# A Fourier-filter and two-layer kernel: the first forward stage as sums and differences in 64-by-64 quarters, three stages' pieces gathered in one step, the second layer two steps behind

## The chip, the cores and the metric

The kernel runs on one core of one Trainium2 chip. The metric is device time in microseconds (us) of one execution; lower is better. "PE" is TensorE, "DVE" VectorE, "ACT" ScalarE, "POOL" GpSimd and "SP" SyncE, which here only issues DMAs.

## The reference

Eight sequences of 3008 rows and 256 columns are filtered in the frequency domain along the rows; the result goes through two matrix products with a PReLU between them.

```
X = np.fft.rfft(x, axis=1)                       # x: 8 x 3008 x 256
y = np.fft.irfft(X * (filt_r + 1j * filt_i), n=3008, axis=1)
h = y.reshape(24064, 256) @ w_in                 # 256 -> 2048
g = np.maximum(h, 0) + alpha * np.minimum(h, 0)
out = g @ w_out                                  # 2048 -> 256
```

## The kernel before

A 3008-point transform is split as 94 times 32. For each batch it has four stages.

- **Stage A** (`piece_a`, L148): a 94-point transform over the rows `n1`. `xs` holds 94 rows on partitions and 8 of the 32 values of `n2`, 256 columns each (a "chunk"; four chunks a batch). One piece is two matmuls (L155) with the stationary 94-by-96 table `wf1_s` and 512 columns each, into one `hps` tile in PSUM, which ACT copies to `asb`. Eight pieces a batch. `save_a` stores a chunk to `a_dram` in HBM, and `turn_a` reads it back transposed into `at`. Both are DMAs on SP's queue.
- **Stage B** (`piece_b`, L172): the 32-point transform as eight matmuls on 64-by-64 quarters of the array (L179), into the PSUM tile `psF`; then on DVE two products with the filter, `ww` (L186) and `uu` (L187). The halves of `ww` are swapped across partitions by four DMAs on POOL's queue: for batch 1 they accumulate straight into `uu` (L191), for later batches they land in `sw` (L193) and `piece_s` adds them on DVE (L198). Six pieces a batch.
- **Stage C** (`piece_c`, L200): the inverse 32-point transform, eight quarter matmuls (L210) into `hps`, copied by ACT to `v`. `turn_c` sends `v` through `v_dram` and reads it as `zt`. Six pieces a batch.
- **Stage D** (`pair_d`, L245): the inverse 94-point transform (L232) into `psF`, copied by ACT to `yT`, the input of the two layers. Eight pieces a batch.

The two layers work on blocks of 512 tokens (one of 384 in twelve). `up(j)` (L474), for 16 values of j, does two matmuls (L479) of the first layer; every second `up` fills an `hps` tile, ACT copies it to `gtb` (L488), and DVE applies the PReLU: two `tensor_scalar` into `m` (L491) and, once in four `up`, one add into `gtb` (L493). `down(q)` is one sixteenth of a block's second layer (a "unit": four matmuls, L510, three for the short block); ACT copies its result to `osb` (L515) and SP stores it (L461).

PSUM: `hps` has two buffers and serves stages A and C and `up`; `psF` has one, for B and D; `op` has two, for `down`. `gtb` is a ring of nine groups of four.

Batch 0 is transformed first, by a class of its own. All else is laid out by hand in 768 steps, one for each `up`. A dictionary `plan` names the pieces that each step does before its `up`; `plan_fft` (L524) fills it for a batch from lists of steps (`a_at`, `b_at`, `c_at`, `d_at` for the pieces, `ta` for `turn_a`, `x_at` for the next batch's loads, which `load_x` puts on POOL's queue). Batch b is filtered while batch b - 1 goes through the layers; stage A of a batch lies beside stages B and C of the batch before. The driver (L582) runs one unit of the block before in each step, after `up`, or before the pieces where the step has an A or C piece (`front`). Every engine executes its instructions in program order.

Of the kernel before, what the change touches and what calls it, by code (L numbers as in the profile page):

```python
# [1 line left out]

# [22 lines left out]
def _build_consts():  # L25

    n1, n2, p = np.arange(N1), np.arange(N2), np.arange(32)
    k1 = (2 * (np.arange(NK) // 2) + 24 * (np.arange(NK) % 2))[None, :] + np.arange(2)[:, None]
    k2 = np.where(p < 16, p, 47 - p)
    g = np.where(p < 16, 1.0, -1.0)  # L30

    a1 = 2 * np.pi * n1[:, None, None] * k1[None] / N1
    wf1 = np.stack([np.cos(a1), -np.sin(a1)], axis=2)
    scale = np.where((k1 == 0) | (k1 == 47), 1.0, 2.0)[None, :, None, :] / NFFT
    wi3 = (wf1 * scale).reshape(N1, 96).T
    wfx = wf1.transpose(0, 3, 1, 2).reshape(N1, 96)
    wf1 = wf1.reshape(N1, 96)

    kk = k1[:, :, None] + N1 * k2
    ang = 2 * np.pi * n2[:, None, None, None] * kk[None] / NFFT  # L40
    c, s = np.cos(ang), np.sin(ang)
    fwd = np.array([[c, -s * g], [s, c * g]])
    twf = fwd.transpose(3, 0, 2, 4, 1, 5).reshape(128, NK, 64)
    inv = np.array([[c, s], [-s * g, c * g]])
    inv = inv.reshape(2, 2, N2, 2, NK // 2, 2, 32).transpose(5, 0, 6, 4, 3, 1, 2)
    inx = np.stack([inv[:, 1], -inv[:, 0]], axis=1)
    return wf1, wfx, wi3, twf, inv.reshape(128, NK, 64), inx.reshape(128, NK, 64)


@with_exitstack  # L50
def kernel(
# [8 lines left out]
    out: bass.AP,  # L60
):
    nc = tc.nc
    names = ("wf1", "wfx", "wi3", "twf", "twi", "twx")
# [20 lines left out]


    wf1_s = konst.tile([N1, 96], FP16, name="wf1_s")
    wfx_s = konst.tile([N1, 96], FP16, name="wfx_s")
    wi3_s = konst.tile([96, N1], FP16, name="wi3_s")
    twf_s = konst.tile([128, NK, 64], FP16, name="twf_s")
# [17 lines left out]
                       ap=[[N2 * D, N1], [1, 8 * D]])  # L107

    def load_x(b, c):
        xs = p_x.tile([N1, 8 * D], FP16, name="xs")  # L110
        for r in (slice(0, 48), slice(48, N1)) :
            nc.gpsimd.dma_start(out=xs[r], in_=xrow(b, c)[r])  # L112
# [25 lines left out]
    class Fft:  # L138
# [3 lines left out]
            self.uw = {}  # L142

        def start_a(self):
            self.asb = p_fft.tile([96, N2, D], FP16, name="asb", tag="asb")
            self.at = p_fft.tile([128, NK, D], FP16, name="at")

        def piece_a(self, i):  # L148
            if i == 0:
                self.start_a()  # L150
            xs = xc[(self.b, i // 2)]
            ps = psH.tile([128, 2, 512], FP32, name="hps")
            for u in range(2):
                o = (i % 2) * 1024 + 512 * u
                nc.tensor.matmul(ps[0:96, u], wf1_s, xs[:, o : o + 512], start=True, stop=True)  # L155
            on_act(self.asb[:, 4 * i : 4 * i + 4].rearrange("p a d -> p (a d)"),
                   ps[0:96].rearrange("p a d -> p (a d)"))

        def save_a(self, c):
            s = slice(8 * c, 8 * c + 8)  # L160
            nc.sync.dma_start(out=a_dram[self.b, :, s], in_=self.asb[:, s])

        def turn_a(self, eng, ka=0, kb=NK):
            for par in range(2):
# [89 lines left out]
    def on_act(o, i):  # L254
        nc.scalar.activation(o, i, AF.Copy)  # L255
# [7 lines left out]
    class First(Fft):  # L263
# [9 lines left out]
        def piece_a(self, i, evict, wide):  # L273
            c, sh = i // 2, i % 2
            ps = banks(wide)
            for f in range(2):
                for u in range(4):
                    o = (4 * sh + u) * D + 128 * f
                    nc.tensor.matmul(ps[:, f, 96 * u : 96 * u + 96], xc[(0, c)][:, o : o + 128], wfx_s,
                                     start=True, stop=True)  # L280
            evict(self.am.rearrange("p (f m s) -> p f m s", f=2, s=N2)[:, :, :, 4 * i : 4 * i + 4],
                  ps[:, :, 0:384].rearrange("p f (s m) -> p f m s", s=4))
# [70 lines left out]
            evict(self.zt[:, 2 * i : 2 * i + 2].rearrange("p a d -> p (a d)"), pt[0:96, 0])  # L353

        def piece_t(self, i, evict):
            pt = banks(i == 4)
            self.turn(pt, i, 4)
            evict(self.zt[:, 4 * i : 4 * i + 4].rearrange("p (h a) d -> p h (a d)", h=2), pt[0:96])

# [43 lines left out]
    for kp in range(12):  # L403
        if kp < 10:
            f0.piece_b(kp + 2)
        if kp == 1:
            nc.vector.memset(twi_s[:, 16:24, 0:1], 0.0)
            tables(nc.sync, ("twi", "twx"), 16, 24)
            nc.sync.dma_start(out=wi3_s, in_=consts["wi3"].ap())
            nc.sync.dma_start(out=al16, in_=moe_alpha.rearrange("(j p) -> j p", p=128))  # L410
            nc.sync.dma_start(out=id32, in_=id32_d.ap())
            nc.sync.dma_start(out=wf1_s, in_=consts["wf1"].ap())
            nc.sync.dma_start(out=sgn_s, in_=sgn_d.ap())
# [105 lines left out]
    plan, front = {}, set()  # L519

    def put(step, fn, *args):
        plan.setdefault(step, []).append((fn, args))

    def plan_fft(b, a_at, ta, quarters, x_at, b_at, add, c_at, d_at):  # L524
        f = Fft(b)
        for i in range(8):
            put(a_at[i], f.piece_a, i)
            front.add(a_at[i])
        for c in range(4):
            put(a_at[2 * c + 1], f.save_a, c)  # L530
            if b + 1 < NB:
                put(x_at[c],
                    lambda b=b, c=c: xc.update({(b + 1, c): load_x(b + 1, c)}))
        for q in range(quarters):
            w = NK // quarters
            put(ta, f.turn_a, nc.sync, w * q, w * q + w)
# [4 lines left out]
        for q in range(6):  # L541
            put(c_at[q], f.piece_c, q)
            front.add(c_at[q])
            if q % 2 == 1:
                put(c_at[q] + 1, f.turn_c, q // 2)
# [22 lines left out]
    def d_steps(p):  # L568
        return [p + t for t in (91, 93, 104, 108, 116, 120, 140, 152)]

    plan_fft(1, range(12, 28, 2), 28, 4, (32, 40, 50, 56), range(36, 72, 6), 0, range(50, 86, 6),
             (94, 95, 98, 101, 111, 121, 142, 154))
    plan_fft(2, (48, 54, 60, 66, 72, 78, 82, 84), 90, 4, (57, 69, 81, 89),
             (106, 116, 126, 136, 148, 158), 7, (116, 126, 136, 148, 158, 172), d_steps(96))
    for b in range(3, NB):
        p = 96 * (b - 1)
        a_at = (10, 16, 22, 28, 34, 36, 44, 48) if b == 3 else (6, 10, 18, 22, 30, 34, 42, 46)
        a_at = [p - 96 + t for t in a_at]
        plan_fft(b, a_at, p - 32, 1, [a_at[2 * c + 1] + 2 for c in range(4)],
                 range(p + 2, p + 74, 12), 8, range(p + 14, p + 86, 12), d_steps(p))  # L580

    prev = None  # L582
    step = 0
    for p, t0, tn, _ in blocks:
        blk = Block(p, t0, tn)
        for j in range(16):
            ahead = step in front and prev is not None
            if ahead:
                prev.down(j)
            for fn, args in plan.pop(step, ()):  # L590
                fn(*args)
            blk.up(j)
# [38 lines left out]
```

## Time and profile before

| what | value |
|---|---|
| median of 3 runs | 783.1 us (782.0 to 789.35) |
| the profiled execution | 783.67 us, its span 781.9 us |
| granted TensorE clock | 0.999 |
| busy: PE, DVE, ACT, POOL | 767.8, 595.4, 587.0, 142.7 us |
| L510 and L479, the two layers | 435.8 and 434.2 us |
| L155, stage A | 33.6 us, 112 matmuls |
| L488 | 385.8 us, 384 instructions |
| L491 and L493 | 233.2 and 231.0 us |
| L186, L187, L198 | 51.1, 51.0, 24.6 us |

The span is the time from the first to the last instruction on the core; the execution's time is 1.8 us more. Busy time is a union over overlapping instructions, so a mean duration times a count can be more than it. For TensorE, whose matmuls overlap, the price of one is best read as the time from its start to the next one's. "Idle before" is the engine's idle time just ahead of an instruction, with what ended it.

### The profile page before, as it was taken

The numbers are of one execution on the slowest core, as the hardware profiler recorded it, in microseconds if no ns is written. First come the engines' busy times: TensorE is split into PE (matmuls) and PEld (weight loads), VectorE is DVE, ScalarE is ACT, GpSimd is POOL, SyncE is SP. The second block draws the span as 40 slices with busy tenths as digits, with TensorE's granted clock in tenths as the row PEclk, the third lists the DMA queues.
The fourth block names the chain that finished last, engine by engine and source line by source line (L and its number), as shares of the span: only waits on it lengthen the run. The fifth ranks groups of instructions, "written<-read, shape, count | busy, mean of one in ns | idle before, by whom it ended". The sixth has DMA issues, their size and how long they took to land.

```text
span 781.9 us, 16069 instructions
## 1 busy us (share of the span) xinstructions
PE 767.8 (98%) x6349; PEld 509.8 (65%) x6349; DVE 595.4 (76%) x1117; ACT 587.0 (75%) x673; POOL 142.7 (18%) x270
## 2 busy tenths in 40 slices
PE   7989999999999999999999999999999999999998
PEld 4646666666666666666666666766666666766666
DVE  3778975788868887787867888688887888666664
ACT  4787786888778877788777887788776877677664
POOL 7520661132102211122201221021111122000000
PEclk9999999999999999999999999999999999999999
DMA  9995799657744657465593565734475233511112
GB/s 171 175 236 149 111 216 219 168 134 173 144 134 101 158 125 152 132 144 114 143 210 80 126 142 126 177 82 108 116 150 135 55 82 95 147 37 28 42 41 54
DMA packets 95179, 100.38 MB, mean 128 GB/s; under 512 B 11184, under 2 KB 83008, under 8 KB 94912
## 3 DMA queue, kind: packets, MB, share of 16 engines
q1 hardware_dynamic: 80480, 69.98, 34.3%
q0 software_dynamic: 14624, 29.38, 21.5%
q8 instruction: 49, 0.80, 0.4%
q14 instruction: 26, 0.21, 0.1%
HBM read 55.28 MB, written 46.66 MB: 130 GB/s over the span
## 4 chain that ended last, share of the span: by engine, by line
PE 94%; DMA 2%; ACT 2%; DVE 1%; POOL 1%; issue 0%; ACTq 0%; POOLq 0%
PE hps L479 41%; PE op L510 41%; PE hps L155 3%; PE psF L232 3%; PE psF L179 2%; PE hps L210 1%; DMA xs<-in_x_dram 1%; ACT gtb L488 1%; DMA zt<-v_dram 1%; ACT v L255 1%; PE psF L347 1%; DMA filt_s<-in_filt_r_dram 0%; POOL xs L112 0%; PE op L325 0%; DVE uu L302 0%
## 5 line engine op out<-in xcount | busy, mean ns | idle before, releaser
L488 ACT ACTIVATE gtb<-hps 128x1024 f16<-128x1024 f32 (+1 forms) x384 | 385.8, 1005 | 133.2 <-PE hps L479 132.4
L510 PE MATMUL op<-wout_s,gtb 128*128 128x256 f16 x3008 | 435.8, 273 | 0.1
L479 PE MATMUL hps<-yT,win_s 128*128 128x512 f16 (+1 forms) x1536 | 434.2, 375 | 1.6 <-ACT gtb L488 1.4
L510 PEld LDWEIGHTS <-gtb 128*128 128x128 f16 x3008 | 293.8, 98 | 168.6 <-issue 0.6
L491 DVE TENSOR_SCALAR m<-gtb,alm_s 128x512 f16<-128x512 f16 (+1 forms) x768 | 233.2, 346 | 149.3 <-ACT gtb L488 148.1
L493 DVE TENSOR_TENSOR gtb<-gtb,m 128x2048 f16<-128x2048 f16 (+1 forms) x192 | 231.0, 1203 | 10.1
L479 PEld LDWEIGHTS <-win_s 128*128 128x128 f16 x1536 | 142.7, 98 | 60.9 <-issue 14.5
L193 POOL DMA_DIRECT2D sw<-ww x144 | 71.2, 502 | 388.5 <-DVE ww L186 377.7
L255 ACT ACTIVATE asb<-hps 96x1024 f16<-96x1024 f32 x56 | 57.1, 1020 | 13.7 <-PE hps L155 13.3
L515 ACT ACTIVATE osb<-op 128x512 f32<-128x512 f32 (+1 forms) x97 | 56.2, 579 | 5.6 <-issue 2.8
L255 ACT ACTIVATE yT<-psF 128x752 f16<-128x752 f32 x59 | 47.0, 797 | 10.0 <-PE psF L232 9.9
L255 ACT ACTIVATE v<-hps 128x1024 f16<-128x1024 f32 (+1 forms) x43 | 43.4, 1010 | 13.6 <-PE hps L210 13.2
L112 POOL DMA_DIRECT2D xs<-in_x_dram x64 | 38.2, 702 | 76.0 <-PE hps L155 69.7
L186 DVE TENSOR_TENSOR ww<-psF,filts_s 128x1024 f16<-128x1024 f32 x42 | 51.1, 1218 | 0.0
L187 DVE TENSOR_TENSOR uu<-psF,filt_s 128x1024 f16<-128x1024 f32 x42 | 51.0, 1215 | 0.0
L155 PE MATMUL hps<-xs,wf_s 94*96 94x512 f16 x112 | 33.6, 381 | 0.6 <-ACT asb L255 0.6
L232 PE MATMUL psF<-wi_s,zt 96*128 96x94 f16 x500 | 31.2, 205 | 1.7 <-DMA zt<-v_dram 1.4
L232 PEld LDWEIGHTS <-zt 96*128 96x128 f16 x512 | 28.5, 98 | 4.8 <-DMA zt<-v_dram 1.7
L191 POOL DMA_DIRECT2D uu<-ww x24 | 19.3, 1229 | 32.9 <-DVE uu L187 27.2
L198 DVE TENSOR_TENSOR uu<-uu,sw 128x1024 f16<-128x1024 f16 x36 | 24.6, 685 | 0.2 <-DMA sw<-ww 0.2
L179 PE MATMUL psF<-at,twf_s 64*64 64x256 f16 x336 | 17.3, 281 | 0.0
L210 PE MATMUL hps<-uu,twi_s 64*64 64x256 f16 x336 | 16.6, 272 | 0.0
(68 smaller groups left out, 168.7 us busy)
## 6 DMA issues: line engine op xcount, KB each, us to landing
out_dram<-osb SPq DMA_DIRECT2D x160, 128.0 KB
a_dram<-asb SPq DMA_DIRECT2D x28, 384.0 KB
v_dram<-v SPq DMA_DIRECT2D x84, 128.0 KB
zt<-v_dram SPq DMA_DIRECT2D x28, 384.0 KB
sw<-ww POOLq DMA_DIRECT2D x144, 64.0 KB, 2.3
at<-a_dram SPq DMA_DIRECT2D x20, 384.0 KB
xs<-in_x_dram POOLq DMA_DIRECT2D x32, 192.0 KB, 4.7
xs<-in_x_dram POOLq DMA_DIRECT2D x32, 184.0 KB, 5.6
```

What stands on the lines that cost most here:

```text
L155: nc.tensor.matmul(ps[0:96, u], wf1_s, xs[:, o : o + 512], start=True, stop=True)
L186: nc.vector.tensor_mul(ww, px, fs)
L187: nc.vector.tensor_mul(uu, px, f)
L193: nc.gpsimd.dma_start(out=sw[o : o + 32], in_=ww[i : i + 32])
L232: nc.tensor.matmul(ps[:, m], self.zt[:, 8 * g + 4 * mh + m, dh * 128 : dh * 128 + 128], wi3_s, start=True, stop=True)
L255: nc.scalar.activation(o, i, AF.Copy)
L479: nc.tensor.matmul(self.hps[:, j % 2, 0:tn], win_s[:, kt, j * 128 : (j + 1) * 128], yT[:, kt, self.t0 : self.t0 + tn], start=(kt == 0), st ...
L488: nc.scalar.activation(g[:, 2 * i : 2 * i + 2], self.hps[:, :, 0:tn], AF.Copy)
L491: nc.vector.tensor_scalar(m[:, 2 * i + h], g[:, 2 * i + h], 0.0, a, OP.min, OP.mult)
L493: nc.vector.tensor_add(g, g, m)
L510: nc.tensor.matmul(self.op[:, si - s0], self.gts[k][:, 128 * si : 128 * si + 128], wout_s[:, k], start=(si == s0 and k == 0), stop=(si == ...
L515: nc.scalar.activation(osb[:, 0:m], self.op[:, 0:m], AF.Copy)
```

## The change

1. **Stage A of batches 2 to 7 is split by parity.** Rows n and n + 47 of the 94-point transform differ only in sign for odd frequencies. `load_halves` loads rows 0 to 46 into a tile `lo` and rows 47 to 93 into another, `hi` (48 rows each, one to spare; two DMAs, on POOL's queue as before). On DVE, `less` writes `lo - hi` to partitions 64 to 110 of `lo`, and `plus` writes `lo + hi` over partitions 0 to 46. `piece_q` then does four matmuls of 512 columns on the four 64-by-64 quarters, with the 47-by-48 tables `wfq_s`: rows 0 to 46 give the even frequencies, rows 64 to 110 the odd, and the two column halves take two of the four `n2` of the piece. The result fills 128 partitions of `hps` in place of 96. `save_q` stores a chunk with two DMAs in place of one. Batch 1 keeps `piece_a`.
2. **The plan is new.** Within a step the order is C, B, A. From batch 3 on, stage A pieces mostly stand in steps that hold a B and a C piece too. The saves come one step later. Each load has three steps in `x_at`: the load, `less` and `plus`.
3. **The driver draws units from a queue.** In a step with n pieces that use `hps` it does n units before the pieces and n after them, and none after `up`; in odd steps away from such pieces it leaves the unit out while the queue holds fewer than 18 - j, so that the second layer falls up to two steps behind and is then drawn ahead.
4. `piece_t(2)` of batch 0 takes an `hps` buffer and `piece_t(4)` a `psF` one, the other way round from before.

```diff
+    def load_halves(b, c):
+        lo, hi = (p_x.tile([128, 8 * D], FP16, name="xs") for _ in range(2))
+        nc.gpsimd.dma_start(out=lo[0:48], in_=xrow(b, c)[0:48])
+        if b + 1 < NB:
+            nc.gpsimd.dma_start(out=hi[0:48], in_=bass.AP(
+                tensor=x.tensor, offset=x.offset + (b * NFFT + 47 * N2 + 8 * c) * D, ap=[[N2 * D, 48], [1, 8 * D]]))
...
+        def less(self, c):
+            lo, hi = xc[(self.b, c)]
+            nc.vector.tensor_tensor(lo[64:111], lo[0:47], hi[0:47], OP.subtract)
+
+        def plus(self, c):
+            lo, hi = xc[(self.b, c)]
+            nc.vector.tensor_tensor(lo[0:47], lo[0:47], hi[0:47], OP.add)
+
+        def piece_q(self, i):
...
+            ps = psH.tile([128, 2, 512], FP32, name="hps")
+            for h in range(2):
+                o = 1024 * h + 512 * u
+                for par in range(2):
+                    r = slice(64 * par, 64 * par + 47)
+                    nc.tensor.matmul(ps[64 * h : 64 * h + 64, par], wfq_s[r], xs[r, o : o + 512],
+                                     start=True, stop=True)
+            on_act(self.asb.rearrange("p (r c w) -> p r c w", r=2, c=4)[:, :, c, 512 * u : 512 * u + 512], ps)
+
+        def save_q(self, c):
+            for h in range(2):
+                nc.sync.dma_start(
...
-            pt = banks(i == 4)
+            pt = banks(i == 2)
...
     def plan_fft(b, a_at, ta, quarters, x_at, b_at, add, c_at, d_at):
         f = Fft(b)
...
+        for q in range(6):
+            put_h(c_at[q], f.piece_c, q)
+            if q % 2 == 1:
+                put(c_at[q] + 1, f.turn_c, q // 2)
         for q in range(6):
             put(b_at[q], f.piece_b, q, not add)
             if add:
                 put(b_at[q] + add, f.piece_s, q)
...
+        for i in range(8):
+            put_h(a_at[i], f.piece_q if x_at else f.piece_a, i)
+        for c in range(4):
+            put(a_at[2 * c + 1] + 1, f.save_q if x_at else f.save_a, c)
+            if x_at:
+                x0, x1, x2 = x_at[c]
+                put(x0, lambda b=b, c=c: xc.update({(b, c): load_halves(b, c)}))
+                put(x1, f.less, c)
+                put(x2, f.plus, c)
...
-    plan_fft(2, (48, 54, 60, 66, 72, 78, 82, 84), 90, 4, (57, 69, 81, 89),
-             (106, 116, 126, 136, 148, 158), 7, (116, 126, 136, 148, 158, 172), d_steps(96))
+    plan_fft(2, (48, 54, 60, 62, 66, 68, 74, 80), 90, 4,
+             ((32, 40, 44), (38, 50, 56), (55, 63, 64), (63, 70, 72)),
+             (106, 116, 126, 136, 148, 158), 7, (116, 126, 136, 148, 158, 170), d_steps(96))
     for b in range(3, NB):
         p = 96 * (b - 1)
-        a_at = (10, 16, 22, 28, 34, 36, 44, 48) if b == 3 else (6, 10, 18, 22, 30, 34, 42, 46)
-        a_at = [p - 96 + t for t in a_at]
-        plan_fft(b, a_at, p - 32, 1, [a_at[2 * c + 1] + 2 for c in range(4)],
+        if b == 3:
+            a_at = (100, 106, 112, 116, 126, 136, 148, 158)
+            x_at = ((70, 88, 97), (84, 102, 109), (108, 119, 123), (118, 130, 142))
+        else:
+            a_at = range(p - 118, p - 22, 12)
+            x_at = [(t - 34, t - 18, t - 6) for t in a_at[::2]]
+            if b == 4:
+                a_at = (170, *a_at[1:])
+        plan_fft(b, a_at, p - 28 if b > 3 else 166, 1, x_at,
                  range(p + 2, p + 74, 12), 8, range(p + 14, p + 86, 12), d_steps(p))
...
+    def pop(n):
+        for _ in range(n):
+            if units:
+                blk, q = units.popleft()
+                blk.down(q)
...
         for j in range(16):
-            ahead = step in front and prev is not None
-            if ahead:
-                prev.down(j)
+            n = psum.get(step, 0)
+            if step < 40:
+                pop(1 if n else 0)
+            else:
+                pop(n)
             for fn, args in plan.pop(step, ()):
                 fn(*args)
+            if step >= 40:
+                pop(n)
             blk.up(j)
-            if prev is not None and not ahead:
-                prev.down(j)
+            if n:
+                last = step
+            else:
+                soon = any(t in psum for t in range(step + 1, step + 14))
+                if not (step >= 40 and step % 2 and step - last > 2 and soon and len(units) < 18 - j):
+                    pop(1)
             step += 1
```

More of the change, by code (lines that the diff above doesn't have):

```diff
@@ L1 @@
+from collections import deque
 from contextlib import ExitStack
@@ L36, in _build_consts @@
     wfx = wf1.transpose(0, 3, 1, 2).reshape(N1, 96)
+    wfq = np.zeros((2, 64, 64))
+    wfq[:, :47, :48] = wf1[:47].transpose(1, 0, 2, 3).reshape(2, 47, 48)
+    wfq = wfq.reshape(128, 64)
     wf1 = wf1.reshape(N1, 96)
@@ L46, in _build_consts @@
     inx = np.stack([inv[:, 1], -inv[:, 0]], axis=1)
-    return wf1, wfx, wi3, twf, inv.reshape(128, NK, 64), inx.reshape(128, NK, 64)
+    return wf1, wfx, wfq, wi3, twf, inv.reshape(128, NK, 64), inx.reshape(128, NK, 64)
 @with_exitstack
@@ L62 @@
     nc = tc.nc
-    names = ("wf1", "wfx", "wi3", "twf", "twi", "twx")
+    names = ("wf1", "wfx", "wfq", "wi3", "twf", "twi", "twx")
     consts = {n: nc.inline_tensor(np.ascontiguousarray(v).astype(np.float16), name="c_" + n)
@@ L86 @@
     wf1_s = konst.tile([N1, 96], FP16, name="wf1_s")
+    wfq_s = konst.tile([128, 64], FP16, name="wfq_s")
     wfx_s = konst.tile([N1, 96], FP16, name="wfx_s")
@@ L109, in load_x @@
     def load_x(b, c):
-        xs = p_x.tile([N1, 8 * D], FP16, name="xs")
-        for r in (slice(0, 48), slice(48, N1)) :
+        xs = p_x.tile([128, 8 * D], FP16, name="xs")
+        for r in (slice(0, 48), slice(48, N1)):
             nc.gpsimd.dma_start(out=xs[r], in_=xrow(b, c)[r])
         return xs
+    def load_halves(b, c):
[5 more added lines that the diff above has]
+        else:
+            nc.gpsimd.dma_start(out=hi[0:32], in_=xrow(b, c)[47:79])
+            nc.gpsimd.dma_start(out=hi[32:47], in_=xrow(b, c)[79:94])
+        return lo, hi
     def load_filt(eng, dst, ha, hb):
@@ L144, in start_a @@
         def start_a(self):
-            self.asb = p_fft.tile([96, N2, D], FP16, name="asb", tag="asb")
+            self.asb = p_fft.tile([128, N2 * D], FP16, name="asb", tag="asb")
             self.at = p_fft.tile([128, NK, D], FP16, name="at")
@@ L154, in piece_a @@
                 o = (i % 2) * 1024 + 512 * u
-                nc.tensor.matmul(ps[0:96, u], wf1_s, xs[:, o : o + 512], start=True, stop=True)
-            on_act(self.asb[:, 4 * i : 4 * i + 4].rearrange("p a d -> p (a d)"),
-                   ps[0:96].rearrange("p a d -> p (a d)"))
+                nc.tensor.matmul(ps[0:96, u], wf1_s, xs[0:N1, o : o + 512], start=True, stop=True)
+            on_act(self.asb[0:96, 1024 * i : 1024 * i + 1024], ps[0:96].rearrange("p a d -> p (a d)"))
         def save_a(self, c):
             s = slice(8 * c, 8 * c + 8)
-            nc.sync.dma_start(out=a_dram[self.b, :, s], in_=self.asb[:, s])
+            nc.sync.dma_start(out=a_dram[self.b, :, s].rearrange("r s d -> r (s d)"),
+                              in_=self.asb[0:96, 2048 * c : 2048 * c + 2048])
+        def less(self, c):
[5 more added lines that the diff above has]
+        def piece_q(self, i):
+            if i == 0:
+                self.start_a()
+            c, u = i // 2, i % 2
+            xs = xc[(self.b, c)][0]
+            ps = psH.tile([128, 2, 512], FP32, name="hps")
[9 more added lines that the diff above has]
+                nc.sync.dma_start(
+                    out=a_dram[self.b, :, 8 * c + 4 * h : 8 * c + 4 * h + 4].rearrange(
+                        "(r k) s d -> k r (s d)", r=2),
+                    in_=self.asb[64 * h : 64 * h + 48].rearrange("p (r c w) -> p r c w", r=2, c=4)[:, :, c])
         def turn_a(self, eng, ka=0, kb=NK):
@@ L278, in piece_a @@
                     o = (4 * sh + u) * D + 128 * f
-                    nc.tensor.matmul(ps[:, f, 96 * u : 96 * u + 96], xc[(0, c)][:, o : o + 128], wfx_s,
+                    nc.tensor.matmul(ps[:, f, 96 * u : 96 * u + 96], xc[(0, c)][0:N1, o : o + 128], wfx_s,
                                      start=True, stop=True)
@@ L412 @@
             nc.sync.dma_start(out=wf1_s, in_=consts["wf1"].ap())
+            nc.sync.dma_start(out=wfq_s, in_=consts["wfq"].ap())
             nc.sync.dma_start(out=sgn_s, in_=sgn_d.ap())
@@ L517, in down, with put_h @@
                         store(self.p, self.t0 + 128 * (s0 + lane), osb, lane)
-    plan, front = {}, set()
+    plan, psum = {}, {}
     def put(step, fn, *args):
         plan.setdefault(step, []).append((fn, args))
+    def put_h(step, fn, *args):
+        put(step, fn, *args)
+        psum[step] = psum.get(step, 0) + 1
     def plan_fft(b, a_at, ta, quarters, x_at, b_at, add, c_at, d_at):
         f = Fft(b)
[L526 to L536, printed above, removed]
+        for q in range(6):
+            put_h(c_at[q], f.piece_c, q)
+            if q % 2 == 1:
+                put(c_at[q] + 1, f.turn_c, q // 2)
         for q in range(6):
@@ L540, in plan_fft @@
                 put(b_at[q] + add, f.piece_s, q)
[L541 to L545, printed above, removed]
+        for i in range(8):
[7 more added lines that the diff above has]
+                put(x2, f.plus, c)
+        for q in range(quarters):
+            w = NK // quarters
+            put(ta, f.turn_a, nc.sync, w * q, w * q + w)
         for i in range(8):
@@ L569, in d_steps @@
         return [p + t for t in (91, 93, 104, 108, 116, 120, 140, 152)]
-    plan_fft(1, range(12, 28, 2), 28, 4, (32, 40, 50, 56), range(36, 72, 6), 0, range(50, 86, 6),
+    plan_fft(1, range(12, 28, 2), 28, 4, None, range(36, 72, 6), 0, range(50, 86, 6),
              (94, 95, 98, 101, 111, 121, 142, 154))
-    plan_fft(2, (48, 54, 60, 66, 72, 78, 82, 84), 90, 4, (57, 69, 81, 89),
-             (106, 116, 126, 136, 148, 158), 7, (116, 126, 136, 148, 158, 172), d_steps(96))
+    plan_fft(2, (48, 54, 60, 62, 66, 68, 74, 80), 90, 4,
+             ((32, 40, 44), (38, 50, 56), (55, 63, 64), (63, 70, 72)),
+             (106, 116, 126, 136, 148, 158), 7, (116, 126, 136, 148, 158, 170), d_steps(96))
     for b in range(3, NB):
         p = 96 * (b - 1)
-        a_at = (10, 16, 22, 28, 34, 36, 44, 48) if b == 3 else (6, 10, 18, 22, 30, 34, 42, 46)
-        a_at = [p - 96 + t for t in a_at]
-        plan_fft(b, a_at, p - 32, 1, [a_at[2 * c + 1] + 2 for c in range(4)],
+        if b == 3:
[7 more added lines that the diff above has]
+        plan_fft(b, a_at, p - 28 if b > 3 else 166, 1, x_at,
                  range(p + 2, p + 74, 12), 8, range(p + 14, p + 86, 12), d_steps(p))
-    prev = None
+    units = deque()
     step = 0
+    def pop(n):
[3 more added lines that the diff above has]
+                blk.down(q)
+    last = 0
     for p, t0, tn, _ in blocks:
@@ L586 @@
         for j in range(16):
-            ahead = step in front and prev is not None
-            if ahead:
-                prev.down(j)
+            n = psum.get(step, 0)
[3 more added lines that the diff above has]
+                pop(n)
             for fn, args in plan.pop(step, ()):
                 fn(*args)
+            if step >= 40:
+                pop(n)
             blk.up(j)
-            if prev is not None and not ahead:
-                prev.down(j)
+            if n:
+                last = step
+            else:
+                soon = any(t in psum for t in range(step + 1, step + 14))
+                if not (step >= 40 and step % 2 and step - last > 2 and soon and len(units) < 18 - j):
+                    pop(1)
             step += 1
         blk.start_down(step == 16 * len(blocks))
-        prev = blk
-    for q in range(16):
-        prev.down(q)
+        units.extend((blk, q) for q in range(16))
+    pop(len(units))
     assert not plan
```

## The prediction

> **What bounds the kernel now.** The first view is the page: the busy shares, and the first line of the chain of work that ended last.
>
> ```profile
> PE 767.8 (98%) x6349; PEld 509.8 (65%) x6349; DVE 595.4 (76%) x1117; ACT 587.0 (75%) x673; POOL 142.7 (18%) x270
> ...
> PE 94%; DMA 2%; ACT 2%; DVE 1%; POOL 1%; issue 0%; ACTq 0%; POOLq 0%
> ```
>
> TensorE is busy 98% of the span and 94% of the chain is its own instructions, so TensorE time taken out comes off the end, as long as nothing else takes its place. DVE's 76% looks like room, but it is a mean over unlike stages. So the second view is busy time by stretch: one while batch 1 goes through stage B (steps 36 to 74; a step is one `up(j)`, and steps were placed in time by counting L479's matmuls), one a steady batch (steps 192 to 288).
>
> ```profile
> core 0: us, PE busy (x) PEld busy (x) DVE busy (x) ACT busy (x) POOL busy (x), PEclk, DMA share, GB/s
> 73.70:115.60 41.90, 41.79 (x348) 25.62 (x348) 36.87 (x61) 32.23 (x37) 24.79 (x34) 1.00 0.84 164
> ...
> 229.60:321.70 92.10, 92.10 (x755) 62.37 (x753) 72.95 (x138) 71.69 (x83) 16.10 (x32) 1.00 0.59 138
> ```
>
> TensorE has no gap in either. DVE is at 36.87 of 41.90 us (88%) in the first and at 72.95 of 92.10 us (79%) in the second. The third view is TensorE's timeline around a stage-A piece and around a step that holds a B and a C piece.
>
> ```profile
> 420.15 0.60 PE L155 MATMUL hps<-xs,wf_s 94*96 94x512 f16 x2
> 420.58 0.60 PE L479 MATMUL hps<-yT,win_s 128*128 128x512 f16 x2
> ```
>
> ```profile
> 427.79 1.04 PE L510 MATMUL op<-wout_s,gtb 128*128 128x256 f16 x8
> 428.75 0.41 PE L179 MATMUL psF<-at,twf_s 64*64 64x256 f16 x8
> 428.99 0.39 PE L210 MATMUL hps<-uu,twi_s 64*64 64x256 f16 x8
> 429.31 1.04 PE L479 MATMUL hps<-yT,win_s 128*128 128x512 f16 x4
> ```
>
> Durations overlap, so the price is start to start: an A piece costs 420.58 - 420.15 = 0.43 us. Eight 64-by-64 matmuls of 256 columns cost 0.24 us (428.75 to 428.99); streamed one after another at the 0.109 us that a 256-column L510 matmul takes they would need 0.87, so four run at once. Going over to quarters costs 0.09 (eight L510 take 0.96 in place of 0.87), coming back 0.1 (L210 takes 0.32, not 0.21). The fourth view is DVE's timeline.
>
> ```profile
> 416.74 0.61 DVE L491 TENSOR_SCALAR m<-gtb,alm_s 128x512 f16<-128x512 f16 x2
> 417.26 1.22 DVE L186 TENSOR_TENSOR ww<-psF,filts_s 128x1024 f16<-128x1024 f32 x1
> 418.39 1.22 DVE L187 TENSOR_TENSOR uu<-psF,filt_s 128x1024 f16<-128x1024 f32 x1
> 419.53 0.61 DVE L491 TENSOR_SCALAR m<-gtb,alm_s 128x512 f16<-128x512 f16 x2
> 420.17 1.22 DVE L493 TENSOR_TENSOR gtb<-gtb,m 128x2048 f16<-128x2048 f16 x1
> ```
>
> Back to back, a tensor-tensor holds DVE 1.14 us (417.26 to 418.39), a pair of L491 0.64.
>
> **The change, part by part.**
>
> *A pieces become quarters (batches 2 to 7, 48 pieces).* Two 512-column matmuls, 0.43 us, become four on the four quarters. No row shows 512 columns there; by L179 (2048 columns in all, the same as here) it is 0.24 us inside a step already in quarters. From the new plan, 42 of the 48 stand in a step with a B or C piece; those at steps 100, 112, 182, 278, 374 and 470 stand alone and pay the change of mode: 0.09 + 0.24 + 0.1 = 0.43, no gain. Unrounded the two are 0.438 and 0.243: 42 x 0.195 = **-8.2 us**. Ends: -9.6 (0.21 a piece), and no overlap of the quarters, which is a rival below.
>
> *Sums and differences (`less`, `plus`).* 48 DVE instructions over 2048 fp16 columns, the shape of L493 but on 47 partitions: 1.14 us each, 54.7 us in all. In steady batches (4 to 7) eight of them, 9.1, go beside 72.95 of 92.1 us; the batch shrinks to about 91, DVE comes to 82, `plus` stands six steps (5.2 us) ahead of its piece and `less` sixteen behind its load. Nothing is left to wait for: 0, with ends 0 and +4 (1 us for each of four batches). Without that cover it would be the whole 9.1 a batch.
>
> *Batch 2, steps 36 to 74.* Here the cover is not there. TensorE's 41.9 us lose five A pieces (2.2), gain six Q pieces (1.5) and about three units of the second layer drawn ahead (3 x 0.44): 42.5. DVE's 36.9 gain four `less` and four `plus`, 9.1: 46.0. So at least 3.5 us must be waited, and the order makes it more, since DVE runs in order and `plus` stands two steps ahead of its piece. Step 66: `plus` (step 64) follows the work of step 63: eviction begins 0.2 after the matmul (timeline at 400.8 and 401.0), takes 1.02 (L488), an L491 pair 0.64, L493 1.14, `plus` 1.22: 4.2 us. TensorE meanwhile has two `up` (0.86), two units (0.88), the change of mode and B (0.33): 2.1. It waits 2.1. Step 74: the same 4.2 against 2.5: 1.7. Step 62: units have run out behind the pieces, so `up` waits for C's eviction, 0.2 + 1.02 less the 0.22 of Q: 1.0. These count no DVE arrears at their start, and stage B leaves some (ww and uu alone take 2.3 at a time). Between 3.5 and 9.1 (all eight paid in full) I take **+8**, near the upper end. Behind each waiting Q stand the step's units and `up`, so ACT, then DVE, run dry as well.
>
> *Batch 3, steps 95 to 137.* Six more `less`/`plus` in some 40 us beside stage B of batch 2; `plus` at step 109 is three steps ahead of its piece at 112 and behind ww and uu of step 106, and D at 111 needs the one psF buffer that uu still holds. Between 0 and 6 x 1.14 = 6.8, **+3**, the middle, since DVE's row for 137 to 178 us is 32.9 of 41 us, less full than batch 2's.
>
> *Held instructions.* `less` writes from partition 64, everything around it from partition 0; DVE's overlap above is 1.22 - 1.14 = 0.08 us a neighbour. [...]
>
> *Loads and saves.* The x loads stay on POOL's queue, 96 rows in place of 94 a chunk, with less time ahead: 8 steps for batch 2's third chunk, 7 for the fourth. Cost 0 if they land in time (rival). Saves become two DMAs of 2 KB pieces on SP's queue, one step later: 24 more issues of 0.3 us on a queue that waits 327 us for `osb`. `turn_a` behind them is read 30 steps later: 0, ends 0 and +1.
>
> *Gathering.* B and C shared steps before, so that part is counted. Drawn-ahead units cover C's eviction (two units 0.88 and Q 0.24 against 1.02 + 0.2); odd steps without a unit leave 1.3 us a pair against ACT's 1.02. 0.
>
> *zt of batch 1.* TensorE waits 1.6 us at 132.8 us for `zt<-v_dram` (step 94). Between its last C (step 80) and step 94 two A pieces (0.87) and four three-matmul units (1.3) go away: 0 to +2.2, **+0.7**, as C itself now comes later against the traffic.
>
> Sum: -8.2 + 8 + 3 + 0.7 = **+3.5 us**. The profiled execution took 783.67 us (span 781.9 and 1.8 around it), 0.6 above the median of 783.1: 783.67 + 3.5 = **787.2 us**, 0.5% above the median. A change under 1% (775.3 to 790.9) is about what a measurement of this kernel cannot tell from none.
>
> **The rivals.**
>
> *DVE hides the sums after all.* For: 24% of DVE is idle, and steady batches fit. Against: 46.0 in 42.5 us. Without waits: 783.67 - 8.2 = 775.5, and 774.5 if the small waits of steps 12 to 40 go too. Chance 0.17.
>
> *`less` waits for its load, and everything behind it on DVE too (slower).* The load of step 55 stands on POOL behind the four accumulate DMAs of step 54.
>
> ```profile
> 96.88 3.19 POOL L191 DMA_DIRECT2D uu<-ww  x4 [1.16 <-PE hps L210]
> 99.01 3.18 POOL L112 DMA_DIRECT2D xs<-in_x_dram  x4
> ...
> DMA to landing us min/median/max: 3.4/5.3/15.0
> ```
>
> From B: DVE arrears 2, ww and uu 2.3, four issues 2.1, its own issue 0.5, landing 5.3 (9.3 for the last of these four, with DMA at 0.84): 12.2 to 16.2 us. DVE comes to `less` at step 63 after nine steps, 9.7 us as measured, and 2 to 3 of arrears: 12. From a landing over 5.3 us it decides; at 9.3 it adds 4, and about as much again at step 70 if not absorbed: 787.2 + 5 = 792. Against: loads with an idle POOL land near 5. Chance 0.22.
>
> *The quarters do not overlap with 47 rows and 512 columns.* With two at a time a piece takes 0.43 again and the 8.2 is lost: 787.2 + 8.2 = 795; one at a time (4 x 0.216 = 0.86), 787.2 + 48 x 0.62 = 817. Against: L179 and L210 show four at once. Chance 0.05.
>
> **How the numbers follow.** Forecast case (779 to 791) 0.54, hidden sums 0.17, late loads 0.22, no overlap 0.05, else 0.02. Range 777 to 797: from just above the no-wait time to all waits at their upper ends (-8.2 + 9.1 + 6.8 + 4 + 2.2 = +13.9). Faster by over 1%: 0.13 (most of the hidden case); slower by over 1%: 0.30 (late loads, no overlap, the forecast's upper end); within 1%: 0.57.
>
> **What would show it.** Q matmuls at 0.24 us start to start between B or C and L510's successor; waits of TensorE for DVE at steps 48 to 74 and 112 of 1 to 3 us each; DVE over 95% busy there; steady batches about 1.1 us shorter than 92.1 us with no wait; `less` at 1.2 us. I am wrong if batch 2's stage A runs without waits of TensorE, if a steady batch is not shorter, or if `less` sits waiting for a DMA.

## The result and the profile after

The changed kernel takes 811.74 us, the median of six runs (809.5 to 812.5), against 783.33 us for six runs of the kernel before. The ratio is 1.0343, 95% interval 1.0308 to 1.0378. It is 28 us slower, not 3.5. Its profiled execution has a span of 807.7 us (before: 781.9) and a mean granted TensorE clock of 0.985 (before: 0.999). On the page, the busy shares and the chain:

```profile
PE 769.2 (95%) x6445; PEld 508.1 (63%) x6445; DVE 649.2 (80%) x1165; ACT 588.4 (73%) x673; POOL 145.5 (18%) x274
...
PE 72%; DMA 12%; DVE 8%; ACT 3%; issue 2%; POOL 2%; SPq 1%; DVEq 0%; ACTq 0%; POOLq 0%
```

Line numbers are from here on those of the changed kernel, except in views of the kernel before: `up` is L525, `down` L556, stage B L224, C L255, D L277, the PReLU L537 and L539, `less` L181, `plus` L185, the quarter piece Q L197, the swap of `ww` into `sw` L238 and the sum with it L243; on SP's queue the save is L203, `turn_a` L213, the store of `v_dram` L266 and the read of `zt` L272.

TensorE is busy as long as before (769.2 against 767.8 us) though the quarters should have made it shorter, and it is now idle for 5% of the span. The chain that was 94% TensorE is 72% TensorE, 12% DMA and 8% DVE. Which DMA and which DVE work, the view of waits says (engine and line, what was waited for: us in all, times, longest):

```profile
PE psF L277 <- DMA zt<-v_dram: 13.0, 4, 4.1
PE hps L197 <- DVE xs L185: 8.4, 5, 4.1
...
SPq L213 <- DMA a_dram<-asb: 30.2, 8, 5.9
```

The 8.4 us of Q for `plus` was forecast in kind. The 13.0 us of stage D (L277) for `zt` was not forecast: only batch 1 had such a wait before, of 1.4 us (the prediction counted it as 1.6), and now four other batches, 2 to 5, have it, of 2.43, 3.73, 2.67 and 4.14 us. The last line is SP's queue: `turn_a` waits for the save in front of it to land.

Busy time by stretch:

```profile
core 0: us, PE busy (x) PEld busy (x) DVE busy (x) ACT busy (x) POOL busy (x), PEclk, DMA share, GB/s
72.90:127.10 54.20, 44.97 (x368) 26.87 (x364) 45.92 (x69) 34.22 (x38) 23.87 (x32) 0.94 0.73 136
...
112.00:118.00 6.00, 5.59 (x24) 3.00 (x24) 4.29 (x8) 2.05 (x2) 2.56 (x5) 0.50 0.39 60
...
323.00:331.00 8.00, 7.97 (x64) 5.67 (x63) 6.68 (x15) 6.13 (x9) 0.52 (x1) 1.00 1.10 209
...
335.00:341.00 6.00, 5.91 (x37) 4.16 (x38) 2.63 (x4) 2.95 (x4) 0.00 (x0) 0.56 0.88 281
...
342.10:435.70 93.60, 90.93 (x754) 59.76 (x752) 81.61 (x144) 72.66 (x83) 15.95 (x32) 1.00 0.58 130
```

Batch 2's stage A (the first row, from step 36 to the Q of step 74) takes 54.2 us, and TensorE has 9.2 us of gaps in it. From the `up` of step 36 to that of step 74 it is 55.4 us, before 41.4. The second and fourth rows are the six microseconds behind two of the waits: the clock is 0.50 and 0.56. The third row is the time ahead of the wait at 331: the DMA engines are full (share 1.10) while TensorE still works. The last row is a steady batch, steps 288 to 384, with one `zt` wait of 2.67 us in it.

A gathered step, and two waits, on TensorE's timeline (start, us, line, operation, idle before):

```profile
450.17 0.41 PE L255 MATMUL hps<-uu,twi_s 64*64 64x256 f16 x8
450.42 0.39 PE L224 MATMUL psF<-at,twf_s 64*64 64x256 f16 x8
450.63 0.39 PE L197 MATMUL hps<-xs,wfq_s 47*64 47x512 f16 x4
450.95 0.50 PE L556 MATMUL op<-wout_s,gtb 128*128 128x256 f16 x3
```

```profile
112.41 0.64 PE L197 MATMUL hps<-xs,wfq_s 47*64 47x512 f16 x4 [4.14 <-DVE xs L185]
...
335.09 0.81 PE L277 MATMUL psF<-wi_s,zt 96*128 96x94 f16 x8 [3.73 <-DMA zt<-v_dram]
```

C, B and Q are 0.25, 0.21 and 0.32 us start to start, the last with the way back to the full array (0.1). Before, B and C alone took 0.24 and 0.32. So Q adds 0.22 us, a little less than the 0.243 forecast: four quarters of 47 rows do run at once.

DVE's timeline at the first of these waits, and in a steady batch:

```profile
108.11 1.22 DVE L181 TENSOR_TENSOR xs<-xs 47x2048 f16<-47x2048 f16 x1 [2.29 <-DMA xs<-in_x_dram]
...
110.00 1.23 DVE L539 TENSOR_TENSOR gtb<-gtb,m 128x2048 f16<-128x2048 f16 x1
111.14 1.21 DVE L185 TENSOR_TENSOR xs<-xs 47x2048 f16<-47x2048 f16 x1
...
350.64 1.22 DVE L539 TENSOR_TENSOR gtb<-gtb,m 128x2048 f16<-128x2048 f16 x1
351.89 1.22 DVE L181 TENSOR_TENSOR xs<-xs 47x2048 f16<-47x2048 f16 x1
353.13 0.62 DVE L537 TENSOR_SCALAR m<-gtb,alm_s 128x512 f16<-128x512 f16 x2
```

At 105.8 `less` of step 63 stands waiting for its x load, for 2.29 us. Behind it on DVE stand the PReLU of the block and `plus`, and behind `plus` Q: TensorE stops for 4.14 us.

Last, SP's queue around the wait at 331, and the same place before. Kernel after:

```profile
310.95 0.91 SPq L203 DMA_DIRECT2D a_dram<-asb  x2
317.60 2.40 SPq L213 DMA_DIRECT2D at<-a_dram  x4
...
322.89 3.57 SPq L266 DMA_DIRECT2D v_dram<-v  x4
330.75 1.73 SPq L272 DMA_DIRECT2D zt<-v_dram  x4
```

Kernel before:

```profile
298.03 3.26 SPq L168 DMA_DIRECT2D at<-a_dram  x4
...
305.19 1.84 SPq L221 DMA_DIRECT2D v_dram<-v  x4
311.46 2.60 SPq L227 DMA_DIRECT2D zt<-v_dram  x4
```

By the trace's DMA packets the read is 3072 packets of 512 bytes, the last `v_dram` store 1024 more. Before, the read of `a_dram` went out 5.7 us ahead of the last C (303.68), and some 2300 of its packets, three quarters, had started when C's result was stored (305.19). After, it goes out 0.4 us behind the last C (317.18), as its save landed late, and only some 1670 have started when the store is issued (322.89). The store must share the full DMA engines with the rest of the read, and `zt` can only be issued 7.9 us after the store (before: 6.3); its data come at 335.04. TensorE has come to D at 331.36.

### The profile page after: what moved, and what is told of

Its sections match the earlier page's. It is cut to its first block, busy times and chain, and to the rows that moved or that the text cites. A ratio compares the mean times of both kernels' runs of the same rounds, so it can differ in the third digit from the quotient of the medians.

```text
span 807.7 us, 16338 instructions
## 1 busy us (share of the span) xinstructions
PE 769.2 (95%) x6445; PEld 508.1 (63%) x6445; DVE 649.2 (80%) x1165; ACT 588.4 (73%) x673; POOL 145.5 (18%) x274
## 4 chain that ended last, share of the span: by engine, by line
PE 72%; DMA 12%; DVE 8%; ACT 3%; issue 2%; POOL 2%; SPq 1%; DVEq 0%; ACTq 0%; POOLq 0%
PE op L556 33%; PE hps L525 31%; PE psF L277 3%; DMA v_dram<-v 2%; DMA at<-a_dram 2%; DVE m L537 2%; DMA zt<-v_dram 2%; ACT gtb L534 2%; DVE gtb L539 2%; PE hps L255 1%; DMA a_dram<-asb 1%; DVE ww L231 1%; PE hps L197 1%; DMA sw<-ww 1%; DVE xs L185 1%
## 5 line engine op out<-in xcount | busy, mean ns | idle before, releaser
L556 PE MATMUL op<-wout_s,gtb 128*128 128x256 f16 x3008 | 436.3, 275 | 0.0
L525 PE MATMUL hps<-yT,win_s 128*128 128x512 f16 (+1 forms) x1536 | 428.3, 377 | 2.7 <-ACT gtb L534 1.2
L556 PEld LDWEIGHTS <-gtb 128*128 128x128 f16 x3008 | 291.6, 98 | 169.5 <-issue 19.2
L537 DVE TENSOR_SCALAR m<-gtb,alm_s 128x512 f16<-128x512 f16 (+1 forms) x768 | 231.9, 346 | 118.4 <-ACT gtb L534 116.3
L539 DVE TENSOR_TENSOR gtb<-gtb,m 128x2048 f16<-128x2048 f16 (+1 forms) x192 | 231.0, 1203 | 10.5
L525 PEld LDWEIGHTS <-win_s 128*128 128x128 f16 x1536 | 147.6, 99 | 58.3 <-issue 7.8
L238 POOL DMA_DIRECT2D sw<-ww x144 | 71.1, 501 | 396.6 <-DVE ww L231 393.7
L300 ACT ACTIVATE asb<-hps 128x1024 f16<-128x1024 f32 (+1 forms) x56 | 57.1, 1021 | 11.1 <-PE hps L197 8.9
L277 PE MATMUL psF<-wi_s,zt 96*128 96x94 f16 x500 | 32.8, 212 | 14.8 <-DMA zt<-v_dram 13.0
L277 PEld LDWEIGHTS <-zt 96*128 96x128 f16 x512 | 29.6, 101 | 22.5 <-DMA zt<-v_dram 14.1
L181 DVE TENSOR_TENSOR xs<-xs 47x2048 f16<-47x2048 f16 x24 | 29.3, 1219 | 2.9 <-DMA xs<-in_x_dram 2.3
L185 DVE TENSOR_TENSOR xs<-xs 47x2048 f16<-47x2048 f16 x24 | 29.0, 1209 | 0.0
L197 PE MATMUL hps<-xs,wfq_s 47*64 47x512 f16 x192 | 19.1, 388 | 8.5 <-DVE xs L185 8.4
L243 DVE TENSOR_TENSOR uu<-uu,sw 128x1024 f16<-128x1024 f16 x36 | 24.5, 682 | 0.4 <-issue 0.4
L122 POOL DMA_DIRECT2D xs<-in_x_dram x24 | 18.1, 752 | 23.1 <-DVE xs L185 20.4
```

Of the source, the lines that this page charges most:

```text
L185: nc.vector.tensor_tensor(lo[0:47], lo[0:47], hi[0:47], OP.add)
L238: nc.gpsimd.dma_start(out=sw[o : o + 32], in_=ww[i : i + 32])
L277: nc.tensor.matmul(ps[:, m], self.zt[:, 8 * g + 4 * mh + m, dh * 128 : dh * 128 + 128], wi3_s, start=True, stop=True)
L525: nc.tensor.matmul(self.hps[:, j % 2, 0:tn], win_s[:, kt, j * 128 : (j + 1) * 128], yT[:, kt, self.t0 : self.t0 + tn], start=(kt == 0), st ...
L537: nc.vector.tensor_scalar(m[:, 2 * i + h], g[:, 2 * i + h], 0.0, a, OP.min, OP.mult)
L539: nc.vector.tensor_add(g, g, m)
```

## The experiments

The runs came in three groups of four, each group on one chip beside the kernel before (783.6 to 783.8 us). "zt waits" are the row `PE psF L277 <- DMA zt<-v_dram`. Each diff is against the changed kernel and shows its main lines alone. The theory after the first reading: the late read of `a_dram` costs most, the sums in batches 2 and 3 the second part. The rivals: the order of issues on SP's queue, the x loads that now lie there, the sums in all batches, or the new driver.

**1. `at_after_zt`**: `turn_a` behind `zt`.

```diff
-        plan_fft(b, a_at, p - 28 if b > 3 else 166, 1, x_at,
+        plan_fft(b, a_at, p - 20 if b > 3 else 172, 1, x_at,
```

> The changed kernel, with turn_a of batches 3 to 7 issued one step after the last turn_c of the batch before it (step p - 20 in place of p - 28; 172 for batch 3), so that the read of a_dram stands behind zt's read on SP's queue. Theory A (the read of a_dram and its wait for the save stand in front of v_dram and zt on SP's queue, and stage D then waits for zt once a batch): the four waits of 2.6 to 4.3 us at 236, 331, 428 and 522 us vanish with the slow clock behind them, about 20 us in all, so 811.7 - 20 = 791 to 793. Theory B (TensorE is only faster between C and D, and zt's two transfers take the time they take): no more than 3 us are gained, 808 or more. If the read then comes too late for stage B, waits of L224 for at would show in place of those for zt.

Measured: 822.2 us, ratio 1.0485 (1.0467 to 1.0503), 10 us more than the changed kernel. The zt waits are gone, so it was this read that held `zt` up. But stage B now waits for `at`, 21.8 us in eight waits: the read, issued at 328.02 us at this place, has a near reader too. The wait only changed places.

**2. `at_on_pool`**: the same step, another queue.

```diff
-            put(ta, f.turn_a, nc.sync, w * q, w * q + w)
+            put(ta, f.turn_a, nc.gpsimd if b > 2 else nc.sync, w * q, w * q + w)
```

> The changed kernel, with turn_a of batches 3 to 7 on POOL's queue at the same steps. The same bytes move at nearly the same time, but SP no longer stands still for the save. Theory A1 (order on SP's queue: v_dram is issued 4 us late behind the blocked read): most of the 20 us come back, 793 to 797. Theory A2 (traffic: the read's small packets hold the DMA engines while v_dram and zt want them): zt stays late by 2 us or more in each batch, 803 to 810. POOL blocked by the save could also hold back sw, which would show as waits of L243 for sw.

Measured: 813.04 us, 1.0375 (1.0354 to 1.0396), 3 us above the range of theory A2; zt waits 13.9 us in four. SP's timeline at the same place:

```profile
319.48 2.73 SPq L266 DMA_DIRECT2D v_dram<-v  x4
332.60 1.73 SPq L272 DMA_DIRECT2D zt<-v_dram  x4
```

The order on SP's queue is not the cause: the store was issued 3.4 us earlier than in the changed kernel, and `zt` 1.9 us later. That leaves the traffic itself, which experiment 9 tests.

**3. `no_sums`**: the halves are loaded straight to partitions 0 and 64 of one tile; `less` and `plus` are left out, so the sums and differences are not computed.

```diff
-                put(x1, f.less, c)
-                put(x2, f.plus, c)
```

> The changed kernel without the sums and differences: rows 0 to 46 and 47 to 93 are loaded straight to partitions 0 and 64 and no less or plus is done, so stage A of batches 2 to 7 works on unsummed rows. Theory: the waits of L197 at steps 48 to 80 and 112, of C at 136 and the arrears behind them are DVE's (46.0 us of work in 42.5), and go: 10 to 13 us, so 799 to 802, while the four waits for zt stay. Rival (the x loads of steps 55 and 63 are what is late): L197 then waits for its load instead, and no more than 4 us are gained, 807 or more.

Measured: 796.88 us, 1.0159 (1.0127 to 1.019), 14.9 us less than the changed kernel and 2 less than the expectation. Steps 32 to 112 (batch 2) take 81.4 us instead of 94.8, the rest of batch 3's stage A 1.4 less. The zt waits stay (13.9 us in four), so they have nothing to do with the sums.

**4. `full_pieces`**: plan and driver as changed, stage A as before in 94-row pieces, without sums.

```diff
-            put_h(a_at[i], f.piece_q if x_at else f.piece_a, i)
+            put_h(a_at[i], f.piece_a, i)
```

> The changed kernel with its new plan and unit queue, but with stage A in full 94-row pieces for all batches (no quarters, no sums; loads at the same steps). By the prices of the trace, 42 pieces cost 0.438 in place of 0.217 us: +9.3 us of TensorE time; the waits for DVE of the no-sums run go, -10 to -13; the waits for zt stay, since stage A stands where it did. So 808 to 811. Rival (the sums cost nothing and quarters are the gain they look): 821.

Measured: 801.54 us, 1.0242 (1.021 to 1.0273), zt waits 13.1 us in five; 6.5 us below the expectation, which priced the quarters at 9.3. So a kernel with nothing of the sums or quarters is 18 us slower than before: the plan, with the driver, is the larger part of the loss. Against `no_sums` the quarters are worth 4.7 us where TensorE also stands waiting.

**5. `a_earlier`**: stage A of batches 4 to 7 twelve steps earlier, its loads with it (batch 4 with steps of its own), `turn_a` four steps earlier; batches 1 to 3 as changed.

```diff
-            a_at = range(p - 118, p - 22, 12)
+            a_at = range(p - 130, p - 34, 12)
...
-        plan_fft(b, a_at, p - 28 if b > 3 else 166, 1, x_at,
+        plan_fft(b, a_at, p - 32 if b > 3 else 166, 1, x_at,
```

> The changed kernel with stage A of batches 4 to 7 ending 12 steps earlier (last piece at p - 46 in place of p - 34) and turn_a at p - 32, as before the change; batches 1 to 3 as in the changed kernel. Theory (the read of a_dram, about 9 us of 512-byte packets on all DMA engines, has to begin some 5 us ahead of the last C, or zt is late): the waits for zt in batches 3 to 6 (3.9, 2.8 and 4.3 us and their slow clock) go, the one of batch 2 (2.6) stays, four more pieces stand alone; 811.7 - 16 + 1 = 795 to 799. Rival (zt is late because C and the gathered step are, whatever the read does): 807 or more.

Measured: 800.1 us, 1.0195 (1.0173 to 1.0216), 11.6 us less than the changed kernel, 1 above the expectation. Of the zt waits of batches 3 to 5 two are left, 0.6 and 0.3 us. But a wait comes up that neither kernel had, `DVE uu L243 <- DMA sw<-ww`, 5.6 us in two, and C behind it.

**6. `quarters_4_to_7`**: as 5, and batches 2 and 3 with the full pieces, loads and steps of before, so without sums where DVE has no room.

```diff
+            put_h(a_at[i], f.piece_q if b > 3 else f.piece_a, i)
...
+    plan_fft(2, (48, 54, 60, 66, 72, 78, 82, 84), 90, 4, (32, 40, 50, 56),
...
+            a_at = (106, 112, 118, 124, 130, 132, 140, 144)
```

> As the run with stage A 12 steps earlier, and batches 2 and 3 with full 94-row pieces, loads and steps as before the change, so that the sums stand only beside batches with room on DVE. If the two causes (DVE in batches 2 and 3, the read's place in batches 3 to 6) are the whole loss, what is left is the gain of some 24 gathered pieces, 24 x 0.22 = 5 us: 777 to 780. If the driver or the order C, B, A costs something of its own: 783 or more.

Measured: 786.57 us, 1.0035 (1.0018 to 1.0052). 25 of the 28 us are gone. It lies in the second branch of the expectation, 783 or more. What shows in its trace is C waiting for `sw` (6.5 us of DVE waits in two), and experiment 11, which moves only the read, takes 4 us more off.

**7. `x_load_later`**: the second chunk's x load, which lay on the save ahead of `turn_a`, 14 steps later.

```diff
+            x_at[1] = tuple(a_at[2] - t for t in (20, 10, 6))
```

> The changed kernel with one x load a batch (second chunk, batches 4 to 7) moved from step p - 32 of the batch before, beside the save and the read of a_dram, to 14 steps later. Theory: part of zt's lateness is this load's traffic, which slows the save that SP waits for: the save lands some 3 us earlier, the read too, and the waits for zt shrink by half or more: 797 to 803. Rival (the read alone is too long for its place): within 3 us of 811.7.

Measured: 812.01 us, 1.0365 (1.0346 to 1.0385), no gain; zt waits 13.2 us in four. The x load is not needed for the wait.

**8. `driver_only`**: steps, full pieces and loads of before (`turn_a` at p - 32); the new driver, the order C, B, A and the saves a step later.

```diff
+        a_at = (10, 16, 22, 28, 34, 36, 44, 48) if b == 3 else (6, 10, 18, 22, 30, 34, 42, 46)
+        a_at = [p - 96 + t for t in a_at]
+        plan_fft(b, a_at, p - 32, 1, old,
```

> The kernel before (its steps, loads and full pieces) under the new driver: units from the queue, order C, B, A, saves one step later. Prices the gathering by itself. Theory: TensorE had no stall to lose in a steady batch, so nothing moves: 781 to 786. Rival (drawing units ahead leaves steps without cover, as at steps 60 to 80): 787 or more.

Measured: 796.66 us, 1.016 (1.0143 to 1.0177), with no zt wait, but 19.3 us of DVE for `sw` and 7.8 us of C behind it. A miss, and a useful one. The three lines, of SP's, POOL's and DVE's timeline:

```profile
293.20 2.27 SPq L213 DMA_DIRECT2D at<-a_dram  x4
...
294.90 1.96 POOL L238 DMA_DIRECT2D sw<-ww  x4 [8.76 <-DVE ww L231]
...
305.45 0.69 DVE L243 TENSOR_TENSOR uu<-uu,sw 128x1024 f16<-128x1024 f16 x1 [4.36 <-DMA sw<-ww]
```

The same read, at the same step as before, is issued 4.8 us sooner (before: 298.03, with `sw` issued at 294.97). It now lies ahead of the swap of `ww` in place of behind it, and `sw` lands 6.9 to 9.5 us after its issue, against 2.2 to 2.7 before. So the read collides on both sides: early with `sw`, late with `zt`.

**9. `half_read`**: the changed kernel, but `turn_a` of batches 4 to 7 reads 12 of the 24 frequencies, and stage B uses them twice: half of the read is left out.

```diff
-                                         twf_s[r, k], self.at[r, k], start=True, stop=True)
+                                         twf_s[r, k], self.at[r, k % 12 if self.b > 3 else k], start=True, stop=True)
...
-            put(ta, f.turn_a, nc.sync, w * q, w * q + w)
+            put(ta, f.turn_a, nc.sync, w * q, w * q + (w if b < 4 else w // 2))
```

> The changed kernel, but turn_a of batches 4 to 7 reads only the first 12 of the 24 frequencies, and stage B uses these twice (the other half of a_dram is left out). Takes away half of the suspected cost and leaves the order on every queue as it is. Theory (the read holds the DMA engines for about 9 us, v_dram and zt come behind it): zt is 4 to 5 us earlier, so the waits in batches 3 to 5 (3.9, 2.8, 4.3 us and the slow clock behind them) go: 811.7 - 16 = 794 to 798. Rival (SP's wait for the save, or the place of the last C, is what makes zt late): 806 or more.

Measured: 794.19 us, 1.0135 (1.0113 to 1.0157), 17.5 us less than the changed kernel, inside the expectation. SP's timeline at the same place:

```profile
316.09 2.22 SPq L213 DMA_DIRECT2D at<-a_dram  x4
...
320.44 2.12 SPq L266 DMA_DIRECT2D v_dram<-v  x4
325.04 1.72 SPq L272 DMA_DIRECT2D zt<-v_dram  x4
```

`zt` follows `v_dram` by 4.6 us, not 7.9. The waits of batches 3 to 5 are all gone; batch 2's (2.42 us at 238), held up by the read of batch 3, which is whole, is left, and 0.3 of batch 1. The three waits (10.5 us) and half of the slow clock's time that is gone, behind batch 2's wait too (6.7), make up 17.2 of the 17.5. Steps 288 to 384 and 384 to 480 take 90.8 and 90.9 us here (92.4 and 92.1 before).

**10. `driver_read_28`**: as 8, with the read four steps later.

```diff
+        plan_fft(b, a_at, p - 28, 1, old,
```

> The driver-only kernel (steps and full pieces of before, new driver) with turn_a at step p - 28 in place of p - 32, so that the last sw of the batch before is issued ahead of the read. Theory (driver-only lost its 12 us because the read, issued 1.7 us ahead of sw, held sw back by 7 us, and L243 with DVE and C behind it waited): the waits of C at 303, 398, 494 and 586 us go, 783 to 787. Rival (the driver costs it by its order of units): 793 or more.

Measured: 785.17 us, 1.0024 (1.0014 to 1.0035). With the read between `sw` and the last C (298.23; `sw` at 293.94, `zt` at 310.61) the 19.3 us of waits are gone. So the driver and the order C, B, A by themselves cost about 2 us, and four steps in the place of one read were worth 11.5.

**11. `quarters_read_28`**: as 6, with the read at p - 28.

```diff
+        plan_fft(b, a_at, p - 28, 1, x_at,
```

> The kernel with quarters in batches 4 to 7 alone (stage A 12 steps earlier there, batches 2 and 3 as before), with turn_a at p - 28 in place of p - 32. Theory: its waits of C for sw at 199, 211 and 577 us (1.0, 2.0, 1.9 us) go, and zt is still in time as it was in the kernel before, where SP also issued the read about there: 778 to 782. If the read now comes too late for zt, waits of L277 show and it stays at 785 or more.

Measured: 782.54 us, 0.9991 (0.9978 to 1.0003): equal to before, and half a us above the expectation. Waits of D for `zt` are back in part, 4.4 us in three.

**12. `quarters_late_driver`**: as 11, and the unit queue used only from step 160, where stage A pieces are quarters.

```diff
-            if step >= 40:
+            if step >= 160:
```

> The same with the old way of drawing units (one ahead of the pieces, one a step) up to step 160 and the queue only after it. Theory: steps 32 to 96 lose about 1 us to the new driver, where units run out; that comes back: 777 to 781, and faster than the kernel before.

Measured: 780.38 us, 0.9952 (0.9934 to 0.9969): 0.5% faster than before and 3.9% faster than the change. Its busy times:

```profile
PE 762.2 (98%) x6413; PEld 505.6 (65%) x6413; DVE 630.9 (81%) x1149; ACT 587.8 (75%) x673; POOL 145.5 (19%) x274
```

TensorE is at 98% again, with 762.2 us of work in place of 767.8: the 5.6 us of the 32 quarters, of which 3.3 us come off the time. DVE's 81% is no longer in the way, as the sums left are those of steady batches.

## Why the prediction was wrong

The prediction failed at the step "`turn_a` behind them is read 30 steps later: 0, ends 0 and +1". It counted the issues and the queue waits and left out what the read occupies: some nine microseconds of all DMA engines (its packets start from 318.5 to about 327.6, at a share of 1.1), and what is due in them. It had asked which queue the DMA stood on, and experiment 2 shows that the queue did not matter. Waits of 12.97 us in batches 2 to 5, and the slow clock behind three of them, stand where it had 0.

**The sum again, with measured terms** (spans, 807.7 - 781.9 = 25.8 us). TensorE's idle time rose by 24.4 us, from 14.1 to 38.5: D waits 13.0 for `zt` where it waited 1.4, Q waits 8.4 for `plus`, and some 4 us are small waits, for `sw` (1.3), for the psF buffer that `uu` holds (1.1) and for C's eviction (1.0) among them. Its busy time rose by 1.4 us: the quarters take off 8.2, and half clock behind four of the waits (6.1, 3.1, 5.2 and 5.1 us) adds 9.7: half of it is lost, as four L556 take 0.86 us start to start there (336.33 to 337.19) and 0.43 at full clock (328.91 to 329.34). By experiments: half the read taken away gives back 17.5 us, the sums 14.9, which with the quarters' -8.2 makes 24.2 of 28.4. Some 4 us are not taken apart by a run of their own; batch 2's `zt` wait (2.4), whose read stayed whole in `half_read`, and the driver's and order's 2 by experiment 10 are of that size.

**Quarters, -8.2: right, and not all of it seen.** A piece adds 0.22 us in a step already in quarters, not 0.43. The rival of no overlap is out. In the time it showed as 4.7 us (experiments 3 and 4), and for 32 of the 48 pieces as 3.3 (12). That waits elsewhere ate the rest is argued, not shown.

**Steady sums, 0: right.** DVE came to 81.61 us a batch (forecast 82), and without the `zt` waits a batch is 1.2 to 1.6 us shorter (forecast 1.1). No `plus` was waited for there.

**Batch 2, +8: the mechanism was right, the term too small.** DVE's work was forecast at 46.0 us and is 45.92, and at step 74 Q waits 1.95 us (forecast 1.7). The sums cost 13.3 us in steps 32 to 112 (experiment 3), beyond the upper bound of 9.1, which took the sums paid in full for the worst: 9.6 of it is idle time of TensorE, the rest longer busy time. Two things were added to the forecast. The rival of late loads came true in one place (2.29 us of `less` at step 63, and Q at step 66 waits 4.14 in place of 2.1), on top of the forecast's waits rather than instead of them; by the prediction's own sign, a `less` that waits for a DMA, this part was wrong. And the clock fell behind that wait. DVE is busy 85% of the stretch, not over 95%, as it runs dry itself while TensorE waits. Batch 3's +3 came to about 1.4.

**Held instructions.** `less`, with its output at partition 64, starts 1.25 us after the L539 before it (350.64 to 351.89), and the next instruction 1.24 us after `less` (353.13), where two neighbours at partition 0 (110.00 and 111.14) are 1.14 apart. It is 0.1 us on each side of `less`, hidden in steady batches.

**zt of batch 1, +0.7: wrong sign.** Its wait, 1.4 us before, is gone.

**Range and rivals.** The slower rivals were about x loads and about the overlap of quarters. None was about a transfer that the change only moves. The range's upper end summed the bounds of the costs it knew of, and so could not hold a cost that was put at nothing.

## What to carry to other kernels

A DMA that is moved in a plan is to be priced by how long it fills the DMA engines, and by which transfers with a near reader are issued in that time: here a read of 3072 packets of 512 bytes, one a batch, was nearly free between the issue of `sw` and the last C (785.17 us, ratio 1.0024), cost 11.5 us over a run when it went out just ahead of `sw`, and at least 17.5 when it went out behind the last C. Where an added instruction meets an engine that has less than its length free, ask also what it waits for, as what stands behind it waits too: here 2.29 us of `less` held the PReLU, `plus` and Q. And a stall of TensorE can cost more than its length: behind four of the five waits of D and Q of 2.43 to 4.14 us here the clock was 0.50 for 3 to 6 us.

## What the runs showed of the hardware that was not expected

**The clock behind a stall.** After the waits of 4.14, 3.73 and 4.14 us that end at 112, 335 and 526 us the granted clock was 0.50 for the next 5 to 6 us, also for work that came without any gap, and then 1.00 again. The 384-column pairs of L525 took 0.49 us before the wait at 331 and 0.85 behind it. A shorter wait did it too: one of 2.43 us at 238 was followed by 0.50 until 241. One of 2.67 at 430.7 was followed by 1.00, and behind the same D's wait of 2.42 in `half_read` eight matmuls of D took 0.51 us, as behind that of 2.67, and not 0.81. The first line is the changed kernel's, the second that of `half_read`:

```profile
238.29 0.81 PE L277 MATMUL psF<-wi_s,zt 96*128 96x94 f16 x8 [2.43 <-DMA zt<-v_dram]
...
238.22 0.51 PE L277 MATMUL psF<-wi_s,zt 96*128 96x94 f16 x8 [2.42 <-DMA zt<-v_dram]
```

So the length of a wait by itself does not tell whether the clock falls behind it; what does was not shown. The prediction had no term for the clock; it was worth about 10 of the 28 us, by the 9.7 of the sum above.

**Two engines' small DMAs in one crowd.** A swap of 2.2 to 2.7 us from issue to landing took 6.9 to 9.5 in `driver_only`, where a strided read went out 1.7 us ahead of it on another engine's queue. The separate queues did not keep the two apart.
